# A recurrent attention and an MLP mixer on one core: the order of every engine's instructions planned inside the kernel instead of by the tile scheduler

## The chip, the cores and the metric

The kernel runs on one NeuronCore of a Trainium2 chip. The metric is the device time of one launch in microseconds (us). A time quoted here is a median over several runs. A run is labelled fast or slow: a run over 1.5% above the fastest run of the same kernel counts as slow, and only fast runs are compared. The time of the whole launch is about 2 us longer than the span of the trace, which begins at the first instruction (235.0 us against 233.0 for the kernel before).

The profile names the engines PE (matrix multiplications), PEld (loading of the stationary operand, overlaps PE), DVE (vector), ACT (scalar, activations), POOL (general purpose) and SP (sync, here only the issue of loads and stores). A name such as L242 is a line of the kernel. `SPq` and `POOLq` mark the issue of DMAs by SP and by POOL.

## The reference, cut to what matters

```python
# q, k, v, f_logit: (batch 4, heads 8, seq 768, head_dim 48), float32
f = 1.0 / (1.0 + np.exp(-f_logit))
for t in range(S):                                     # a recurrence over 768 positions
    state = f[:, :, t, :, None] * state + np.einsum('bhd,bhe->bhde', k[:, :, t], v[:, :, t])
    y[:, :, t] = np.einsum('bhd,bhde->bhe', q[:, :, t], state)

x = y.transpose(0, 2, 1, 3).reshape(B, S, 384)         # heads side by side
h = np.maximum(x.transpose(0, 2, 1) @ w_tok1, 0.0) @ w_tok2      # token mixing: 768 -> 256 -> 768
u = x + h.transpose(0, 2, 1)
return u + np.maximum(u @ w_ch1, 0.0) @ w_ch2          # channel mixing: 384 -> 1536 -> 384
```

Both kernels cut the sequence into six chunks of 128 positions. For each of the 24 pairs of batch and chunk they compute gates (exponentials and logarithms of `f_logit`), cumulative sums, the decayed q and k, scores within the chunk, a readout and an update of the state: this is called attention below. When all six chunks of a batch are read out, its mixing can start: two token matmul groups (12 matmuls with `w_tok1`, called the token matmuls below), then the matmuls with `w_tok2`, transposes, 72 matmuls with `w_ch1` and 72 with `w_ch2`. Attention of batch b+1 runs among the mixing of batch b.

## The kernel before

The parts that the change and the argument touch. The tile framework decides the order of each engine's instructions from the order in which they are emitted and from priorities; dependencies are found by it too.

```python
q_sb = two([128, H, NCH, D], BF16, "q_sb")            # two buffers each, used by batch b % 2
f_sb = two([128, H, NCH, D], FP32, "f_sb")            # likewise k_sb, v_sb

def load_f(b, eng, c=None):                           # one chunk, or all six in one DMA
    i = b % 2
    if c is None:
        eng.dma_start(out=f_sb[i], in_=tview(f_logit, b))
    else:
        eng.dma_start(out=f_sb[i][:, :, c, :], in_=tview(f_logit, b)[:, :, c, :])

def gates(b, c0, c1):                                 # three activations on ACT
    ...
    nc.scalar.activation(fb, fb, AF.Exp, bias=0.0, scale=-1.0)                            # L127
    nc.scalar.activation(Lhi[i][:, c0:c1, :, 0:D], fbc, AF.Ln, bias=1.0, scale=1.0)       # L128
    nc.scalar.activation(fb, fb, AF.Ln, bias=1.0, scale=1.0)                              # L129
    eng = nc.gpsimd if b else nc.vector
    eng.tensor_tensor(Llo[i][:, c0:c1, :, 0:D], fbc, Lhi[i][:, c0:c1, :, 0:D], ALU.subtract)   # L131

def readout(b, c):
    ...
    nc.scalar.copy(x_nat[i][:, c, :], py[:, 0:DM])
    (nc.gpsimd if b else nc.vector).tensor_copy(x_bf[i][:, c, :], x_nat[i][:, c, :])      # L187

# ... (front, scores, update, mixing: see the whole kernel)

for c in range(NCH):
    load_f(0, nc.sync, c)
for c in range(NCH):
    load_qkv(0, c)                                    # on POOL's queue, chunk by chunk
for w, src in ((w_tok1, moe_w_tok1), (w_tok2, moe_w_tok2), (w_ch1, moe_w_ch1), (w_ch2, moe_w_ch2)):
    nc.gpsimd.dma_start(out=w, in_=src.rearrange("(kt p) n -> p kt n", p=128))
load_f(1, nc.gpsimd)                                  # L279: whole batch, behind the weights
load_qkv(1)                                           # whole batch

for c in range(NCH):
    gates(0, c, c + 1)                                # all gates of batch 0 first on ACT
front(0, 0)
scores(0, 0)
front(0, 1)
for n, (b, c) in enumerate(steps):
    ...                                               # attention of one chunk, and a share of the
                                                      # mixing of the batch before among it
```

## Time and profile before

Four runs of the kernel before have a median of 232.71 us (230.48 to 234.62). The profiled execution took 235.0 us and counts as slow by the rule above, at a mean granted clock of 0.993, so no difference of less than about 2 us is read from its trace.

| stretch of the trace before | what limits it | PE busy |
|---|---|---|
| 0 to 45 us | loads, and in-order ACT with all gates of batch 0 first (the first decay exponential runs at 14.94 us) | 1.15, 2.77, 6.91, 8.01 us in the first four 10 us |
| 45 to 61 us | the `f_logit` load of batch 1, then what hangs on it | 1.12 us in 50 to 60 |
| from about 90 us | PE itself | nearly 10 us in each 10 us |

The head of the profile of the kernel before: busy tenths of each engine in 40 slices of 5.8 us, the granted clock of PE, and the busy share of the 16 DMA engines.

```profile
span 233.0 us, 4447 instructions
PE   0125778501379669999999999999999999999994
PEclk9999999999999997999999999999999999999999
DMA  8999999999999990009996000121000021100022
DMA packets 90292, 19.94 MB, mean 86 GB/s; under 512 B 80896, under 2 KB 89616, under 8 KB 90272
```

The hole in the PE row at slices 8 to 11 is the stall. The DMA engines are busy all the time until 87 us, with small packets: 90,292 packets for 19.94 MB. A load that is issued into this traffic lands late: `f_logit` of batch 1, issued behind the weights, takes 29.2 us from issue to landing.

The windows view of the kernel before. The columns are the stretch, its length, the busy us and instruction counts of PE, PEld, DVE, ACT and POOL, the granted clock, the DMA share and GB/s.

```profile
30.00:40.00 10.00, 8.01 (x79) 4.38 (x78) 6.47 (x18) 7.59 (x16) 1.76 (x1) 1.00 1.16 210
40.00:50.00 10.00, 4.25 (x42) 2.51 (x41) 5.96 (x16) 3.19 (x6) 0.00 (x0) 1.00 1.37 204
50.00:60.00 10.00, 1.12 (x13) 0.82 (x13) 2.63 (x1) 7.19 (x10) 6.78 (x4) 1.00 2.41 110
60.00:70.00 10.00, 6.51 (x60) 4.00 (x59) 5.56 (x10) 4.25 (x11) 7.00 (x4) 1.00 1.81 165
```

The chain of waits that ended last in the kernel before, in order of time: start, length, and what it was.

```profile
21.57 0.96 POOL w_ch_77 L278
22.53 29.18 DMA f_sb_85<-in_f_logit_dram
51.74 1.58 ACT f_sb_85 L127 x2
...
57.37 3.74 DVE x_bf_110 L187
...
79.99 0.66 PE pm L242 x3
...
117.47 0.97 PE pm L219 x6
...
159.50 0.97 PE pm L219 x6
...
199.04 1.96 PE pm L219 x12
...
229.70 0.55 DVE out_sb_119 L256
```

One DMA, `f_logit` of batch 1, stands in the chain for 29.18 us. It was issued behind the four weights on POOL's queue. The gates on ACT follow it, then a cast on DVE that takes 3.74 us. L242 at 79.99 us is the first channel matmul. L219 are the token matmuls of batches 1, 2 and 3: they mark the pace, 42 and 40 us per batch.

The list of waits of the kernel before in the stretch 30 to 80 us has the same load: total, times, longest.

```profile
ACT f_sb_85 L127 <- DMA f_sb_85<-in_f_logit_dram: 8.0, 1, 8.0
```

The timeline of DVE and of POOL around the slow cast, both of the kernel before:

```profile
57.37 3.73 DVE L187 CAST x_bf_110<-x_nat_108 128x384 bf16<-128x384 f32 x1 [9.91 <-ACT x_nat_108 L186]
57.64 4.95 POOL L131 TENSOR_TENSOR Llo_89<-f_sb_85,Lhi_87 128x768 bf16<-128x768 f32 x3
```

Alone the same cast takes 0.36 us, so beside three subtractions on POOL it takes ten times as long. Two multiplications of DVE, at 83.57 and 85.28 us, take 1.79 us each beside the next subtractions on POOL (81.80 to 88.57 us), and 0.36 us each alone. By what mechanism POOL's work slows DVE's is not shown.

### The profile page before, as it was taken

Reading aid. Unit: us, or ns where it says so; the run is one execution under the profiler, and the core shown is the slowest. Engines: PE = TensorE matmul, PEld = TensorE weight load, DVE = VectorE, ACT = ScalarE, POOL = GpSimd, SP = SyncE. Lnnn points to the kernel's source line nnn. Section 1 sums busy time; section 2 is a strip of 40 time slices with the busy share of each in tenths; the row PEclk is TensorE's granted clock in tenths of the full one; section 3 lists DMA queues with packets and bytes.
Section 4 is the critical chain, followed back from the end, with each engine's and each line's share of the span. In section 5 each row is a group of like instructions: output and inputs, shape, how many; then the busy total and the mean of one; then the engine's idle time right before and its main releaser. Section 6 shows DMA issues by size and latency. Waiting matters only on the chain.

```text
span 233.0 us, 4447 instructions
## 1 busy us (share of the span) xinstructions
PE 184.3 (79%) x1768; PEld 113.9 (49%) x1768; DVE 136.5 (59%) x283; ACT 114.8 (49%) x250; POOL 85.3 (37%) x115
## 2 busy tenths in 40 slices
PE   0125778501379669999999999999999999999994
PEld 0013445301245445666665666666665666455662
DVE  4145757711668796576668767756877762444221
ACT  5662394519254963762346774224766511165300
POOL 9979230008950596258245221201621221220000
PEclk9999999999999997999999999999999999999999
DMA  8999999999999990009996000121000021100022
GB/s 119 149 139 170 170 214 204 226 149 93 131 193 140 78 97 4 0 28 147 200 107 32 3 0 4 68 70 68 3 0 3 0 70 69 68 3 0 2 103 101
DMA packets 90292, 19.94 MB, mean 86 GB/s; under 512 B 80896, under 2 KB 89616, under 8 KB 90272
## 3 DMA queue, kind: packets, MB, share of 16 engines
q0 software_dynamic: 77472, 11.41, 78.9%
q1 hardware_dynamic: 12800, 8.26, 15.2%
q8 instruction: 14, 0.23, 0.5%
q14 instruction: 6, 0.05, 0.1%
HBM read 25.17 MB, written 4.72 MB: 128 GB/s over the span
## 4 chain that ended last, share of the span: by engine, by line
PE 60%; DMA 18%; ACT 7%; DVE 7%; POOL 6%; issue 1%; DVEq 0%; ACTq 0%; POOLq 0%
PE pm L242 20%; PE pm L253 18%; DMA f_sb_85<-in_f_logit_dram 13%; PE pm L226 4%; DMA k_sb_80<-in_k_dram 4%; PE pm L219 3%; ACT uT L236 3%; PE pq L158 2%; DMA out_dram<-out_sb_119 2%; PE pk L162 2%; ACT f_sb_85 L127 2%; DVE x_bf_110 L187 2%; POOL q_sb_78 L120 2%; PE py L178 1%; PE pd L196 1%; PE pS L139 1%
## 5 line engine op out<-in xcount | busy, mean ns | idle before, releaser
L242 PE MATMUL pm<-uT,w_ch_76 128*128 128x384 bf16 x288 | 55.1, 330 | 2.4 <-DVE zT L246 2.3
L253 PE MATMUL pm<-w_ch_77,zT 128*128 128x384 bf16 x288 | 50.6, 326 | 0.0
L248 ACT ACTIVATE zT<-pm 128x384 bf16<-128x384 f32 x56 | 27.5, 492 | 23.9 <-PE pm L242 23.8
L253 PEld LDWEIGHTS <-zT 128*128 128x128 bf16 x288 | 27.0, 98 | 16.7
L242 PEld LDWEIGHTS <-w_ch_76 128*128 128x128 bf16 x288 | 26.1, 98 | 17.9 <-issue 3.8
L246 DVE TENSOR_SCALAR zT<-pm 128x384 bf16<-128x384 f32 x40 | 21.2, 552 | 7.8 <-PE pm L242 7.5
L158 PE MATMUL pq<-ident,qh_94 128*128 128x128 bf16 x48 | 5.9, 249 | 11.3 <-DVE qh_94 L150 11.3
L146 ACT ACTIVATE G_90<-pS 128x384 bf16<-128x384 f32 x12 | 5.9, 488 | 15.2 <-PE pS L145 12.5
L219 PE MATMUL pm<-x_bf_110,w_tok_74 128*128 128x384 bf16 x24 | 7.2, 419 | 7.4 <-DVE x_bf_110 L187 6.4
L226 PE MATMUL pm<-h1T,w_tok_75 128*128 128x384 bf16 x48 | 12.2, 354 | 0.7 <-ACT h1T L221 0.5
L186 ACT COPY x_nat_109<-py 128x384 f32<-128x384 f32 x12 | 5.8, 482 | 12.9 <-PE py L183 11.8
L236 ACT CAST uT<-pm 128x384 bf16<-128x384 f32 x24 | 10.2, 488 | 3.6 <-PE pm L234 3.5
L118 POOL DMA_DIRECT2D k_sb_81<-in_k_dram x2 | 4.4, 2210 | 20.3 <-issue 20.3
L163 DVE CAST qkT_98<-pk 128x512 bf16<-128x512 f32 x12 | 8.3, 689 | 5.8 <-PE pk L162 5.8
L207 POOL CAST state_bd_106<-state_104 48x192 bf16<-48x192 f32 x9 | 3.1, 342 | 23.1 <-DVE state_104 L205 8.9
L138 PE MATMUL pS<-Lhi_87,tri_bf 128*128 128x384 bf16 x12 | 4.4, 371 | 8.8 <-ACT Lhi_87 L128 8.8
L187 DVE CAST x_bf_110<-x_nat_108 128x384 bf16<-128x384 f32 x6 | 5.5, 919 | 10.1 <-ACT x_nat_108 L186 9.9
L146 ACT ACTIVATE G_91<-pS 128x384 bf16<-128x384 f32 x12 | 5.8, 485 | 10.0 <-PE pS L145 10.0
L187 POOL CAST x_bf_111<-x_nat_109 128x384 bf16<-128x384 f32 x12 | 6.0, 503 | 12.5 <-ACT x_nat_109 L186 12.3
L158 PEld LDWEIGHTS <-qh_94 128*128 128x128 bf16 x48 | 3.8, 110 | 13.0 <-DVE qh_94 L150 11.9
L131 POOL TENSOR_TENSOR Llo_89<-f_sb_85,Lhi_87 128x768 bf16<-128x768 f32 x6 | 9.9, 1671 | 0.1
L234 PE MATMUL pm<-ident,u_bf 128*128 128x128 bf16 x72 | 7.5, 218 | 3.1 <-ACT uT L236 1.8
(217 smaller groups left out, 411.5 us busy)
## 6 DMA issues: line engine op xcount, KB each, us to landing
out_dram<-out_sb_118 SPq DMA_DIRECT2D x12, 192.0 KB, 1.9
out_dram<-out_sb_119 SPq DMA_DIRECT2D x12, 192.0 KB, 1.9
f_sb_84<-in_f_logit_dram SPq DMA_DIRECT2D x6, 192.0 KB, 5.5
w_ch_76<-in_moe_w_ch_dram POOLq DMA_DIRECT2D x1, 1152.0 KB, 18.8
w_ch_77<-in_moe_w_ch_dram POOLq DMA_DIRECT2D x1, 1152.0 KB, 23.9
f_sb_85<-in_f_logit_dram POOLq DMA_DIRECT2D x1, 1152.0 KB, 29.2
q_sb_79<-in_q_dram POOLq DMA_DIRECT2D x2, 576.0 KB, 17.3
k_sb_81<-in_k_dram POOLq DMA_DIRECT2D x2, 576.0 KB, 10.2
```

The lines of the kernel that those rows point to most:

```text
L131: eng.tensor_tensor(Llo[i][:, c0:c1, :, 0:D], fbc, Lhi[i][:, c0:c1, :, 0:D], ALU.subtract)
L146: nc.scalar.activation(G[j].rearrange("t h d -> t (h d)"), Sv, AF.Exp, bias=0.0, scale=-1.0)
L158: nc.tensor.matmul(pq[:, hp * 128:(hp + 1) * 128], lhsT=qb[:, hp, :], rhs=ident, start=True, stop=True)
L163: nc.vector.tensor_copy(qkT[j][:, 4:8, :], pk.rearrange("p (a t) -> p a t", a=4))
L187: (nc.gpsimd if b else nc.vector).tensor_copy(x_bf[i][:, c, :], x_nat[i][:, c, :])
L219: nc.tensor.matmul(pm[:, 0:DM], lhsT=w_tok1[:, kt, rt * 128:(rt + 1) * 128], rhs=x_bf[i][:, kt, :], start=(kt == 0), stop=(kt == NCH - 1))
L226: nc.tensor.matmul(pm[:, 0:DM], lhsT=w_tok2[:, kt, tt * 128:(tt + 1) * 128], rhs=h1T[:, kt, :], start=(kt == 0), stop=(kt == 1))
L236: nc.scalar.copy(uT[:, :, tt * 128:(tt + 1) * 128], pm[:, 0:DM].rearrange("p (m t) -> p m t", m=3))
L242: nc.tensor.matmul(pm[:, 0:384], lhsT=w_ch1[:, kt, cc * 128:(cc + 1) * 128], rhs=uT[:, kt, th * 384:(th + 1) * 384], start=(kt == 0), stop ...
L246: nc.vector.tensor_scalar(dst, pm[:, 0:384], 0.0, None, ALU.max)
L248: nc.scalar.activation(dst, pm[:, 0:384], AF.Relu, bias=0.0, scale=1.0)
L253: nc.tensor.matmul(pm[:, 0:DM], lhsT=zT[:, kt, tt * 128:(tt + 1) * 128], rhs=w_ch2[:, kt, :], start=(kt == 0), stop=(kt == NCC - 1))
```

## The change

The intent: the kernel lists all operations with the engines that may do them, an assumed duration, their dependencies and a key (a wished time). A small list scheduler inside the kernel then simulates the engines, PSUM banks and one serial DMA queue, and gives one order. The instructions are emitted in that order with the tile scheduler's reordering switched off (`tc.manual_schedule()`). The framework still inserts the semaphores. Along with it come other changes: q, k, v and f_logit are loaded chunk by chunk for every batch, the layout of their tiles has the chunk outermost, gates alternate with attention, most casts go to DVE or ACT instead of POOL, and `w_ch2` is loaded after five chunks of batch 1 (`W2 = 5`).

The diff, cut to its core:

```diff
+class Plan:
+    LATE = {"PE": 0.32, "ACT": 0.24, "DVE": 0.24, "POOL": 0.3, "SP": 0.1, "Q": 2.0}   # visible to others after
+    BANKS = {"att": 5, "mix": 3}
+    def add(self, engines, fn, key, deps=(), bank=None, frees=None, at=0.0, banks=1): ...
+    def order(self):
+        queues = {e: sorted((o for o in self.ops if e in o["eng"]), key=lambda o: o["key"])
+                  for e in ("PE", "ACT", "DVE", "POOL", "SP", "Q")}
+        ...                      # again and again: the operation that can start first, ties by key
-    q_sb = two([128, H, NCH, D], BF16, "q_sb")
-    f_sb = two([128, H, NCH, D], FP32, "f_sb")
+    q_sb = two([128, NCH, H, D], BF16, "q_sb")
+    f_sb = two([128, NCH, H, D], FP32, "f_sb")
+    def load_f(b, c, key, at=0.0):
+        i = b % 2
+        deps = [made.get(("lo", b - 2, c))]            # the last reader of this buffer
+        if b:
+            def token(e):                              # makes the load wait for DVE's place in the order
+                nc.vector.memset(f_sb[i][0:1, c, 0, 0:1], 0.0)
+            deps = [add({"DVE": 0.06}, token, key, deps, at=at)]
+        def issue(e):
+            nc.sync.dma_start(out=f_sb[i][:, c], in_=chunk_of(f_logit, b, c))
+        n = add({"SP": 0.1}, issue, key, deps, at=at)
+        made["f", b, c] = add({"Q": 1.1}, None, key, [n])        # 1.1 us on a serial queue
+    def load_qkv(b, c, key, at=0.0):
+        ...                                            # POOL 0.89 us to issue, 0.72 us on the queue
+    def gates(b, c0, c1, key):
+        ...
+        o = add({"POOL": 0.85 * n} if b > 1 else {"DVE": 0.4 * n + 0.08},
+                lambda e: on(e).tensor_tensor(lo, fb, hi, ALU.subtract), key, [g, h])
+    def attention(b, c, key, at=0.0):
+        p2 = (b, c - 2) if c >= 2 else (b - 1, c + NCH - 2)      # the last user of these buffers
+        ...
+            made["bd", b, c] = add({"DVE": 0.5, "ACT": 0.5}, diag, key + 0.02, [s_, made.get(("y", *p2))])
+        ...
+        made["xb", b, c] = add({"DVE": 0.28, "ACT": 0.4}, ...)   # was POOL from batch 1 on
-    load_f(1, nc.gpsimd)
-    load_qkv(1)
+    W2 = 5
+    PACE = (34.0, 5.6)
+    for c in range(NCH):
+        load_f(0, c, 0.1 * c)
+        load_qkv(0, c, 0.1 * c)
+    ...                                                # w_tok1, w_tok2, w_ch1
+    for c in range(NCH):
+        if c == W2:
+            load_w("w_ch2", w_ch2, moe_w_ch2, 0.63 + 0.01 * c, 6.0)
+        load_f(1, c, 0.63 + 0.01 * c, at=24.0 + 2.0 * c + (6.0 if c >= W2 else 0.0))
+        load_qkv(1, c, 0.63 + 0.01 * c)
+    for c in range(NCH):
+        gates(0, c, c + 1, 0.1 * c)
+        attention(0, c, 0.1 * c + 0.1)
+    for b in range(B):
+        if b + 1 < B:
+            for c in range(NCH):
+                if b >= 1:
+                    load_f(b + 1, c, b + 0.05 + 0.1 * c)
+                    load_qkv(b + 1, c, b + 0.05 + 0.1 * c)
+            ...                                        # gates and attention of batch b + 1
+        mixing(b, b + 1.0, 1.0)
+    order = plan.order()
+    with tc.manual_schedule():
+        for t, e, o in order:
+            if o["fn"] is not None:
+                o["fn"](e)
```

## The prediction

> **What bounds the kernel now.** Three stages.
>
> (1) Start, 0 to 45 us. The windows view shows PE 1.15, 2.77, 6.91 and 8.01 us busy in the first four 10 us windows. ACT works in order and has all six gate groups of batch 0 first, so the first decay exponential runs at 14.9 us and PE's first transposes at 15.9 us, though q, k, v take only about 8 us to land.
>
> (2) A stall, 45 to 61 us: PE busy 1.12 us in 50 to 60. The chain of waits names it: the f_logit load of batch 1, one DMA behind the four weights on POOL's queue, takes 29.2 us and lands at 51.7; ACT has been idle for 8.0 us in front of it; then five 128x768 gate activations, then an x_bf cast on DVE that takes 3.73 us (0.36 alone) while three Llo subtractions take 4.95 us on POOL. [...] (qh_95 and kh_97 also take 1.7 us beside POOL, 0.36 alone). Mixing of batch 0 is late by all this.
>
> (3) From about 90 us PE is the limit: busy 98 to 100% of each window to 200 us. Batches follow at 42 and 40 us (token matmuls at 117.5, 159.5, 199.0 in the chain).
>
> **What the change does.** PE's work stays. In dense stretches three channel matmuls take 0.49 us, twelve 1.95: 28.4 us of mixing per batch (estimate: 174 matmuls at 0.163 plus transposes), and attention about 2.0 us per chunk ((81.6 - 2x28.4)/12). Sum 162 us.
> - Gates are interleaved with the chunks: batch 0 attention starts about 5 us sooner.
> - f_logit of batch 1 comes by chunk on SP's queue, so ACT is not blocked: stage (2), about 16 us, goes.
> - q, k, v of batch 1 come by chunk before w_ch2. Bytes and small packets stay; the DMA row is full until 87 us now. [...] So channel matmul 2 of batch 0 cannot start before about 60 us.
> - x_bf, u_bf and state_bd casts leave POOL for DVE or ACT: some 7 us per batch, where DVE and ACT are 67% and 50% busy in 120 to 200.
> - Steady state gains little: PE was full already; 0 to 2 us a batch.
>
> **Sum.** Token matmuls of batch 0 end at about 37 us (62 now), its channel matmuls begin at 41 to 43 (80 now), token matmuls of batch 1 at 75 to 80 (117.5 now). Then about 109 us of PE work (4 left over, 85 mixing, 20 attention), some 6 us of gaps and 3 us of output tail: about 197 us, 16% less. Chances: faster 0.95, same 0.03, slower 0.02.
>
> **What would show it.** No ACT wait of more than 3 us for batch 1's f_logit; PE at least 70% busy in 40 to 60; first channel matmul near 42 us; batch periods still 39 to 42 us; PE busy sum falling to 170 to 180.
>
> **What would make it wrong.** The order is fixed by assumed durations and serial DMA. If loads land later (f_logit of batch 2 is issued early and competes with q, k, v of batch 0), in-order engines block on the wrong instruction: slower, to 210. If w_ch2 lands after 65 us PE idles. If attention of batch 0 ends at 30 us: below 190.

75 to 80 us, then 109, 6 and 3 us, come to 193 to 198 us, put at about 197. The 60 us for channel matmul 2 rest on the full DMA row alone and are the author's estimate.

## The result, and the profile after

The changed kernel takes 216.91 us (median of four runs, 215.31 to 217.47), the kernel before 232.71 us. The ratio is 0.934, with a 95% interval from 0.924 to 0.944. A ratio in this document is the mean time of one kernel's fast runs over that of the other's fast runs of the same rounds, so it is not quite the ratio of the quoted medians. The change is faster, by 6.6%, but the predicted 197 us are missed, and so are the 210 us that the prediction gave for loads that land later.

The head of the profile of the changed kernel, to be read against the one above:

```profile
span 215.3 us, 4558 instructions
PE   0525789588999597978989999998999999899993
PEclk9999999976999889996999999999999999999999
DMA  7999999999999999999979002210000132000032
DMA packets 106326, 19.96 MB, mean 93 GB/s; under 512 B 100288, under 2 KB 105920, under 8 KB 106304
```

The long hole of PE is gone. But the DMA row stays full until about 118 us instead of 87 us, in one piece. There are 16,000 more packets for the same 20 MB: the loads by chunk bring all of `f_logit` in pieces of 192 bytes, where before that held for batch 0 alone, and the others came in pieces of 768 or 4,224 bytes. The clock row has new dips.

The windows view of the changed kernel:

```profile
30.00:40.00 10.00, 8.37 (x87) 5.13 (x85) 6.83 (x22) 7.09 (x18) 1.97 (x3) 1.00 1.31 179
40.00:50.00 10.00, 7.06 (x54) 4.04 (x55) 6.36 (x19) 6.76 (x17) 4.38 (x5) 0.81 1.78 136
50.00:60.00 10.00, 10.00 (x106) 5.76 (x105) 8.25 (x23) 8.59 (x23) 4.50 (x5) 0.85 1.72 136
...
70.00:80.00 10.00, 7.53 (x66) 4.40 (x64) 4.77 (x12) 4.03 (x10) 4.38 (x5) 0.83 1.97 143
```

Between 40 and 60 us PE is busy for 17.06 us, against 5.37 us before. Part of that is the same work done slowly: the granted clock is 0.81 to 0.85 in three of the four stretches shown (the trace before has 1.00 in its four, but its clock records begin only at 74.5 us). And there is a new weak stretch from 70 to 80 us.

The chain of waits of the changed kernel:

```profile
6.16 11.41 DMA v_sb_82<-in_v_dram
...
23.93 13.63 DMA w_ch_76<-in_moe_w_ch_dram
37.84 16.27 DMA k_sb_81<-in_k_dram
54.41 19.22 DMA w_ch_77<-in_moe_w_ch_dram
73.68 2.10 PE pm L452 x6
...
83.18 1.72 DVE state_108 L335
...
97.47 3.73 PE pm L384 x12
...
141.34 1.97 PE pm L384 x12
...
181.95 1.31 PE pm L384 x7
...
211.91 0.55 DVE out_sb_123 L461
```

Up to 73.68 us most of the chain is four loads, one behind another; the chain before had the 29.18 us load and, at the start, a load of k of 8.47 us. `w_ch2` (`w_ch_77`) lands at 73.6 us, where the prediction had about 60. The token matmuls of batch 1 (L384) start at 97.47 us, 20 us sooner than before, but at 75 to 80 in the prediction. From there to the end it takes 117.8 us of trace (215.3 less 97.5); before it was 115.5 (233.0 less 117.5), and the prediction's sum has 118. So the whole miss of 20 us lies before the token matmuls of batch 1.

What stood at 73 us, in the list of waits of the changed kernel for 60 to 80 us:

```profile
ACT G_90 L272 <- PE pS L266: 5.2, 1, 5.2
DVE qh_94 L281 <- ACT G_90 L272: 4.1, 1, 4.1
...
PE pm L452 <- DMA w_ch_77<-in_moe_w_ch_dram: 2.5, 1, 2.5
```

PE waits for `w_ch2` for only 2.5 us. But behind that matmul in PE's fixed order stands the cumulative sum of batch 1, chunk 4 (it starts at 75.58 us), and ACT waits 5.2 us for it, and DVE 4.1 us: with a fixed order one late load stops attention too, which did not need it. PE is also at half its clock here (granted 0.50, in a record of 3.4 us from 73.5 us on): the first six matmuls with `w_ch2` take 2.10 us, where six take about 0.98 us later.

Who kept the DMA engines busy? The timeline of SP, of the changed kernel: the issue of `f_logit` loads, `f_sb_84` being batches 0 and 2, `f_sb_85` batches 1 and 3.

```profile
0.75 33.30 SPq L211 DMA_DIRECT2D f_sb_84<-in_f_logit_dram  x11
34.10 3.44 SPq L211 DMA_DIRECT2D f_sb_85<-in_f_logit_dram  x1
37.64 2.06 SPq L211 DMA_DIRECT2D f_sb_84<-in_f_logit_dram  x1
39.76 33.80 SPq L211 DMA_DIRECT2D f_sb_85<-in_f_logit_dram  x11
```

By 34 us SP has issued eleven loads of `f_sb_84`: six of batch 0 and five of batch 2, which ACT first uses at 79.1 us. By 73.5 us batch 3 is issued as well. Of these twelve loads of batches 2 and 3 (1,024 packets of 192 bytes each) seven are issued before `w_ch2` is, at 54.4 us, and beside the q, k, v loads of batches 0 and 1; the other five are issued while `w_ch2` is under way. The plan allows it: as soon as the gates have used a chunk of `f_sb`, the next but one batch may be loaded into it, SP is idle, and the plan's single serial queue has holes.

### The profile page after: what moved, and what is told of

It is laid out like the page before. It is cut to its first block, busy times and chain, and to the rows that moved or that the text cites. A ratio compares the mean times of both kernels' runs of the same rounds, so it can differ in the third digit from the quotient of the medians.

```text
span 215.3 us, 4558 instructions
## 1 busy us (share of the span) xinstructions
PE 182.8 (85%) x1768; PEld 112.8 (52%) x1768; DVE 134.7 (63%) x317; ACT 141.7 (66%) x315; POOL 77.5 (36%) x90
## 2 busy tenths in 40 slices
DMA packets 106326, 19.96 MB, mean 93 GB/s; under 512 B 100288, under 2 KB 105920, under 8 KB 106304
## 4 chain that ended last, share of the span: by engine, by line
PE 52%; DMA 28%; DVE 6%; ACT 5%; POOL 5%; issue 2%; DVEq 0%; POOLq 0%
PE pm L452 21%; PE pm L433 16%; DMA w_ch_77<-in_moe_w_ch_dram 9%; DMA k_sb_81<-in_k_dram 8%; DMA w_ch_76<-in_moe_w_ch_dram 6%; DMA v_sb_82<-in_v_dram 5%; PE pm L384 3%; POOL k_sb_80 L228 2%; PE pm L403 1%; DVE u_nat_118 L407 1%; POOL q_sb_78 L228 1%; POOL v_sb_82 L228 1%; PE pk L292 1%; PE pq L292 1%; ACT u_bf L189 1%
## 5 line engine op out<-in xcount | busy, mean ns | idle before, releaser
L452 PE MATMUL pm<-w_ch_77,zT 128*128 128x384 bf16 x288 | 53.3, 331 | 2.5 <-DMA w_ch_77<-in_moe_w_ch_dram 2.5
L433 PE MATMUL pm<-uT,w_ch_76 128*128 128x384 bf16 x288 | 53.0, 330 | 0.0
L195 ACT ACTIVATE zT<-pm 128x384 bf16<-128x384 f32 x78 | 37.9, 503 | 4.1 <-PE pm L433 3.8
L433 PEld LDWEIGHTS <-w_ch_76 128*128 128x128 bf16 x288 | 26.7, 98 | 16.1 <-issue 0.7
L461 DVE TENSOR_TENSOR out_sb_122<-u_nat_118,pm 128x384 f32<-128x384 f32 x6 | 3.3, 550 | 17.5 <-PE pm L452 17.4
L228 POOL DMA_DIRECT2D k_sb_80<-in_k_dram x12 | 10.7, 888 | 9.1 <-DMA w_ch_77<-in_moe_w_ch_dram 6.5
L228 POOL DMA_DIRECT2D k_sb_81<-in_k_dram x12 | 10.8, 898 | 8.7 <-DMA w_ch_76<-in_moe_w_ch_dram 5.3
L228 POOL DMA_DIRECT2D v_sb_83<-in_v_dram x12 | 10.8, 903 | 5.7 <-DMA q_sb_79<-in_q_dram 4.2
L228 POOL DMA_DIRECT2D q_sb_79<-in_q_dram x12 | 10.9, 912 | 4.3 <-DMA k_sb_81<-in_k_dram 2.4
L228 POOL DMA_DIRECT2D q_sb_78<-in_q_dram x12 | 10.9, 906 | 3.7 <-DMA k_sb_80<-in_k_dram 1.3
L228 POOL DMA_DIRECT2D v_sb_82<-in_v_dram x12 | 10.7, 896 | 3.5 <-DMA q_sb_78<-in_q_dram 1.4
L197 DVE TENSOR_SCALAR zT<-pm 128x384 bf16<-128x384 f32 x18 | 9.6, 551 | 3.2 <-PE pm L433 3.0
L189 ACT COPY x_nat_112<-py 128x384 f32<-128x384 f32 x11 | 5.3, 478 | 9.3 <-PE py L352 8.5
L384 PEld LDWEIGHTS <-w_tok_74 128*128 128x128 bf16 x48 | 5.2, 114 | 7.4 <-issue 6.0
L189 ACT COPY x_nat_113<-py 128x384 f32<-128x384 f32 x9 | 4.4, 492 | 6.8 <-PE py L352 6.8
L407 DVE TENSOR_TENSOR u_nat_118<-x_nat_113,pm 128x384 f32<-128x384 f32 x12 | 6.1, 546 | 3.9 <-PE pm L403 3.9
```

Source lines behind the costliest of these rows:

```text
L189: nc.scalar.copy(dst, src)
L195: nc.scalar.activation(dst, src, AF.Relu, bias=0.0, scale=1.0)
L197: nc.vector.tensor_scalar(dst, src, 0.0, None, ALU.max)
L228: lambda e, dst=dst, src=src: nc.gpsimd.dma_start(out=dst[i][:, c], in_=chunk_of(src, b, c)),
L384: nc.tensor.matmul(t["p"][:, 0:DM], lhsT=w_tok1[:, kt, rt * 128:(rt + 1) * 128], rhs=x_bf[i][:, kt, :], start=(kt == 0), stop=(kt == NCH - 1))
L407: u = made["u", b, tt] = add({"DVE": 0.47}, lambda e, tt=tt, t=t: nc.vector.tensor_tensor(u_nat[i][:, tt, :], x_nat[i][:, tt, :], t["p"][: ...
```

## The experiments

The theories are named as the expectations name them. Theory A: the early `f_logit` loads of batches 2 and 3 take DMA time from what is needed next. Its rivals: B, PE's slow matmuls at the start and the latency of the chain of chunks cost the time (in the changed kernel 384-column matmuls are 0.29 to 0.32 us apart before 35.9 us and 0.162 us later; the texts call this the cold or slow clock, but the trace has no clock record before 35.9 us); C, `w_ch2` is simply placed too late (`W2 = 5`); D, POOL's subtractions slow DVE down (1.7 us for an operation that takes 0.36 us alone). A further question is what part of the gain comes from the fixed order and what part from the rest, such as the loads by chunk. Every edit of the kernel makes the plan anew, so the order of operations that were not edited can change with it. Twelve runs were made, in three batches on three chips. Where kernels of different batches are compared, it is by their ratios to the kernel before.

| kernel | median us (lowest, highest) | ratio to before | correct |
|---|---|---|---|
| changed kernel | 216.91 (215.31, 217.47) | 0.934 | yes |
| 1 late f_logit loads | 208.72 (206.20, 209.65) | 0.890 (two fast runs) | yes |
| 2 w_ch2 first | 217.91 (215.69, 218.90) | 0.9348 | no |
| 3 the same again | 219.19 (one run) | | no |
| 4 w_ch2 first, dependency added | 214.96 (213.03, 216.07) | 0.9218 | yes |
| 5 order left to the tile scheduler | 224.52 (223.65, 225.52) | 0.9647 | yes |
| 6 kernel before, f_logit of batch 1 on SP | 234.16 (232.53, 235.26) | 1.0054 | yes |
| 7 f_logit in whole batches | 224.09 (223.38, 225.01) | 0.9618 | yes |
| 8 run 1, subtractions on DVE | 206.74 (205.69, 207.10) | 0.8864 | yes |
| 9 run 8, f_logit of batch 0 paced | 205.56 (205.32, 206.36) | 0.8832 | yes |
| 10 run 9, PE kept busy | 205.71 (204.41, 212.59) | 0.8811 | yes |
| 11 run 9, dependency added | 207.39 (206.88, 207.81) | 0.8901 | yes |
| 12 run 9, order left to the tile scheduler | 217.99 (217.41, 218.40) | 0.9355 | yes |

In the second and third batch (runs 4 and 7 to 12; run 3 is a single run and has no verdict) the recorded verdict reads "unclear" although the intervals of the ratios, about 0.006 to 0.011 to either side, lie far from 1; two of the seven runs of the kernel before were classed slow there. For run 1 two of its four runs count as slow (209.37 and 209.65 us); 0.890 is the mean of its two fast runs (207.1 us) over the mean of the six fast runs of the kernel before in that batch (232.8 us).

### Run 1: the f_logit loads of batches 2 and 3 later

```diff
-                    load_f(b + 1, c, b + 0.05 + 0.1 * c)
+                    load_f(b + 1, c, b + 0.05 + 0.1 * c, at=(52.0 if b == 1 else 76.0) + 3.2 * c)
```

> Only change: the f_logit loads of batches 2 and 3 are held until the time at which the plan itself serves them (52 us and 76 us plus 3.2 us a chunk), instead of being issued by SP as soon as their buffer is free (from 6 us on). Theory A (early f_logit loads steal packets from q, k, v of batches 0 and 1 and from w_ch2): the last token matmul of batch 0 comes at 38 to 40 us (41.9 in the changed kernel), w_ch2 lands before 67 us (73.6), PE does not wait for it, and the time is 207 to 211 us (216.9). Rival B (the slip is the cold PE clock and the latency of the chunk chain, not the order of loads): within 1.5 us of 216.9.

Measured: 208.72 us, ratio 0.890, so 8 to 10 us faster than the changed kernel. The last token matmul of batch 0 runs at 38.1 us instead of 41.9, the first channel matmul at 45.73 instead of 51.16, the first with `w_ch2` at 64.92 instead of 73.68, with no wait for it. Its chain of waits has hardly a load left. By engine, the changed kernel's chain and then that of run 1:

```profile
PE 52%; DMA 28%; DVE 6%; ACT 5%; POOL 5%; issue 2%; DVEq 0%; POOLq 0%
```

```profile
PE 59%; DVE 22%; ACT 9%; DMA 4%; issue 3%; POOL 2%; DVEq 0%; POOLq 0%
```

DMA falls from 28% of the chain to 4%. PE's first 481 operations of 1,768, up to about 60 us, are the same in both traces, so the 4 and 5 us gained by then do not come of another order on PE; after that the orders differ. What follows: theory A holds, and it is the largest single piece of the miss. The rival B, which expected no more than 1.5 us, is not the main cause. The token matmuls of batch 1 begin at 86.09 us, so half of the lateness against the predicted 75 to 80 goes, half stays.

### Runs 2, 3 and 4: w_ch2 in front of batch 1

```diff
-    W2 = 5
+    W2 = 0
```

> Only change: w_ch2 is issued before all q, k, v loads of batch 1 instead of before those of chunk 5. If the place of w_ch2 alone costs what the prediction lost (theory C), PE no longer waits for it near 71 us and the time falls to 210 to 213 us. Theory A says the total of DMA packets is what counts: w_ch2 lands by 52 us, but q, k, v of batch 1 land 10 us later, attention of batch 1 is late, and the time is 215 to 222 us.

Measured: 217.91 us, no gain, and a wrong result, with a relative error of 0.0619. `w_ch2` is no longer waited for, but q, k, v and f_logit of batch 1 come later by as much: the first transposes of batch 1 run at 57.4 us instead of 48.5. So the place of `w_ch2` alone is not the fault: theory C expected 210 to 213 us. Too much traffic in front of either load would explain it.

The wrong result was not expected. First, whether it is a chance event:

> The same kernel as e2, once more, only to see whether its wrong result comes again. A fault in the kernel that this order brings out would come again; a rare event would not. Time 215 to 219 us.

The error came again, the same to the last digit, at 219.19 us. So it is fixed by the order, not by timing. Comparing the order with the list of dependencies showed what is missing: `state_bd` has two buffers; the cast of chunk c writes buffer c % 2, and the readout of chunk c reads buffer (c - 1) % 2. So before the cast of chunk c writes, the readout of chunk c - 1 must have read that same buffer. The plan lists the readout of chunk c - 2 instead. In the order of the changed kernel the right sequence happens to hold everywhere; with `W2 = 0` the cast comes before the readout for batch 2, chunk 2, and for batch 3, chunk 0. The check for races cannot find this: with a fixed order the emitted sequence is the meaning of the program, and the semaphores then keep the wrong sequence faithfully.

```diff
-            made["bd", b, c] = add({"DVE": 0.5, "ACT": 0.5}, diag, key + 0.02, [s_, made.get(("y", *p2))])
+            made["bd", b, c] = add({"DVE": 0.5, "ACT": 0.5}, diag, key + 0.02,
+                                   [s_, made.get(("y", b, c - 1) if c else ("y", b - 1, NCH - 1))])
```

> e2 (w_ch2 before the loads of batch 1) plus one dependency that the plan's list lacks: the cast into state_bd of chunk c waits for the readout of chunk c-1, which still reads the tile's older value. e2's plan puts that cast in front of the readout twice (batch 2 chunk 2, batch 3 chunk 0); the changed kernel's never does. If this is why e2 gave a wrong result, e11 is correct. Time as e2: 215 to 220 us.

Measured: correct, 214.96 us, ratio 0.9218. The missing dependency is the cause. The ratio lies 0.012 under that of the changed kernel, with intervals that overlap (0.911 to 0.933 and 0.924 to 0.944): not told apart.

### Run 5: the changed kernel without the fixed order

```diff
-    with tc.manual_schedule():
-        for t, e, o in order:
-            if o["fn"] is not None:
-                o["fn"](e)
+    for t, e, o in order:
+        if o["fn"] is not None:
+            o["fn"](e)
```

> The changed kernel with the same loads, layouts, engines and order of emission, but without the fixed order: the tile scheduler may move instructions again. If the fixed order is what gives the gain over the kernel before, this falls back to 225 to 233 us. If the gain comes from the split loads and the order of emission, it stays within 3 us of 216.9.

Measured: 224.52 us, ratio 0.9647. This is neither of the two times expected, but near the first. So of the 6.6% gain about 3.5% stay without the fixed order (loads by chunk, layout, engines, order of emission), and about 3.1%, some 7 us, are lost with it. The fixed order therefore has a part in the gain. But it fixes two things, the order of compute and the time at which loads are issued, and this run lets both go: by 30 us it has issued 16 loads of `f_logit` where the changed kernel has issued ten, and `w_tok1` lands at 41.7 us instead of 29.1. Run 12 comes back to this.

### Run 6: the kernel before, with only f_logit of batch 1 moved to SP's queue

```diff
-    load_f(1, nc.gpsimd)
+    load_f(1, nc.sync)
```

> The kernel before with one line changed: f_logit of batch 1 is issued on SP's queue (right after batch 0's) instead of last on POOL's. Theory A: the stall of 45 to 61 us, whose start is this load, shrinks by about 8 us of ACT wait; q, k, v of batch 0 come some 2 us later; the time is 222 to 228 us, so a third to two thirds of the gain of the change is this one load. Rival: q, k, v of batch 1 are then the next thing to be late on the same DMA engines, and the time stays at 230 to 233 us.

Measured: 234.16 us, ratio 1.0054 (0.997 to 1.014): no gain. The load that the chain named as the stall no longer stalls, and the kernel is as slow as ever. Its chain of waits shows who pays:

```profile
6.12 12.14 DMA v_sb<-in_v_dram
18.55 16.21 DMA k_sb<-in_k_dram
...
40.52 16.75 issue
```

The early load on the other queue now delays q, k, v of batch 0 and all that is behind them on POOL's queue. That is not the whole of it: the 16.75 us of "issue" are a time in which POOL stands at its loads of batch 1 for a reason that the profile does not show, and POOL's subtractions of batch 1 start only after it, at 59.5 us. The kernel before has such a wait too, of 20.3 us. What it costs here was not tested. The pages of the profile count both queues on the same 16 DMA engines (in the kernel before POOL's takes 78.9% and SP's 15.2% of those engines' time), and in run 6 POOL's queue falls to 1,026 packets in 5 us beside SP's, from 7,338 alone in run 1. Counting the profile's packets in the traces:

| kernel and stretch | POOL's queue, packets of 96 B | SP's queue, packets |
|---|---|---|
| run 1, 15 to 20 us, POOL's queue alone | 7,338 | none |
| changed kernel, 45 to 50 us | 2,730 | 2,153 of 192 B |
| changed kernel, 50 to 55 us | 2,542 | 2,235 of 192 B |
| run 6, 15 to 20 us | 1,026 | 1,035 of 768 B |
| run 7, 35 to 40 us | 1,029 | 1,042 of 768 B |

In these stretches the two queues go nearly packet for packet: 1.1 to 1.3 of POOL's to one of 192 bytes, one to one with those of 768 bytes (the kernel before has 618 to 618 in 22 to 25 us). By what rule they do so is not shown. An estimate from these counts: a q, k or v chunk (1,024 packets) that takes 0.7 us alone (5 us x 1,024 / 7,338) takes about 2.0 us beside 192-byte pieces and 5 us beside 768-byte pieces. The plan had 0.72 us for it, and one queue in which the loads come strictly after each other.

### Run 7: f_logit of batches 1 to 3 in one DMA each

```diff
-    f_sb = two([128, NCH, H, D], FP32, "f_sb")
+    f_sb = two([128, H, NCH, D], FP32, "f_sb")
...
+            if b:
+                nc.sync.dma_start(out=f_sb[i], in_=f_logit[b].rearrange("h (c t) d -> t h c d", t=C))
+            else:
+                nc.sync.dma_start(out=f_sb[i][:, :, c, :], in_=chunk_of(f_logit, b, c))
```

> The changed kernel with f_logit of batches 1 to 3 loaded in one DMA each, in the layout of the kernel before (768-byte packets there, 192-byte packets in the changed kernel), still issued as soon as the buffer is free. If the number of small packets is what the early loads cost (theory A2), 13,800 packets fewer bring as much as holding the loads back did (8 us): 207 to 211 us, w_ch2 before 67 us. If only the early issue matters, it stays at 214 to 218 us.

Measured: 224.09 us, ratio 0.9618, so 3.0% slower than the changed kernel where a gain was expected if the 192-byte pieces were the fault, and outside both of the times expected. There are fewer packets, but POOL's queue moves fewer of its own beside them (1,029 in 5 us in the last line of the table above, 2,542 to 2,730 beside those of 192 bytes), and a whole batch has to land before its first chunk can be used: ACT waits 6.2 us for `f_logit` of batch 1 again. So joining the small pieces is no cure in this form. How much the number of pieces costs by itself this run cannot say, since it changed three things at once: their size, when the first chunk can be used, and when the buffer is free for the load. Run 1 has the same 106,326 packets as the changed kernel and is 8 to 10 us faster: there only the time at which they are sent was edited.

### Run 8: run 1, and the subtraction Llo of batches 2 and 3 on DVE

```diff
-        o = add({"POOL": 0.85 * n} if b > 1 else {"DVE": 0.4 * n + 0.08},
+        o = add({"DVE": 0.4 * n + 0.08},
```

> e1 (late f_logit loads) plus: the Llo subtractions of batches 2 and 3 run on DVE (0.88 us planned) instead of POOL (1.7 us). If POOL's subtraction slows the DVE operations beside it (1.7 us instead of 0.36) and this is on the chain at 85 and 95 us (theory D), it is 2 to 4 us faster than e1 (208.7): 205 to 207 us. Rival: DVE, 66% busy, only takes more work, and the time is within 1 us of e1 or above.

Measured: 206.74 us, ratio 0.8864, against 0.890 of run 1's two fast runs. The medians differ by 2.0 us, the ratios by less than 1 us. What theory D supposes is visible in the traces (a state update of the changed kernel at 83.18 us takes 1.72 us beside a subtraction on POOL, 0.36 us at 103.06), but its worth in time is not settled by these runs; it is at most about 2 us.

### Run 9: run 8, and f_logit of batch 0 paced

```diff
-        if b:
+        if b or at:
...
-        load_f(0, c, 0.1 * c)
+        load_f(0, c, 0.1 * c, at=2.6 * c if c > 1 else 0.0)
```

> e7 plus: the f_logit loads of batch 0's chunks 2 to 5 are issued at 5 to 13 us instead of all at once at the start. If they delay q, k, v of the first chunks by sharing the DMA engines (theory A at the start), the last token matmul of batch 0 moves from 38.1 us in e1 to 36 or 37 us and the time is 1 to 3 us below e7. Rival: all 24 loads of batch 0 are needed in any order before the last chunk can start, so nothing changes (within 1 us).

Measured: 205.56 us (205.32 to 206.36), ratio 0.8832 (0.876 to 0.890), correct. This is the fastest version: 11.7% under the kernel before, and 5.1% of that kernel's time under the changed kernel. The last token matmul of batch 0 runs at 36.8 us, as expected. Against run 8 of the same batch it gains 1.2 us of median with overlapping spreads, so the rival (within 1 us) is not excluded. The head of its profile:

```profile
span 203.2 us, 4569 instructions
PE   0787887799999999678999999989999998899993
DMA  8999999999999999999970022100001122000132
```

PE works from the second slice on. The DMA row is as full as before, until about 110 us: it is the same traffic, in an order in which the next thing needed comes next.

### Run 10: run 9, with PE kept busy

Before each PE operation of batch 0's attention stand four more 128x128 matmuls whose result is never used.

```diff
+    def heat(b):
+        if b == 0:
+            ...
+            for _ in range(4):
+                nc.tensor.matmul(warm[0][:, 0:128], lhsT=ident, rhs=ident, start=True, stop=True)
```

> e9 plus four matmuls of 128x128 into an unused bank in front of each PE operation of batch 0's attention, which keep PE busy while it waits for loads. If the slow clock of the first 35 us (384-column matmuls 0.3 us apart instead of 0.16) costs time (rival B), the last token matmul of batch 0 moves from 36.8 us to 34 to 36 us and the time is 1 to 3 us below e9 (205.6). If loads set the pace there, it is within 1 us of e9 or slower.

Measured: 205.71 us, ratio 0.8811: the same as run 9. The matmuls did become faster: the timeline of PE has the first seven token matmuls of batch 0, in run 9 and in run 10 in turn, as

```profile
28.32 2.42 PE L384 MATMUL pm<-x_bf,w_tok 128*128 128x384 bf16 x7
```

```profile
28.73 1.31 PE L398 MATMUL pm<-x_bf,w_tok 128*128 128x384 bf16 x7
```

so 1.31 us instead of 2.42 us. But the last two of them start at 36.05 us instead of 36.52 us. So keeping PE busy in this way gains nothing that can be measured in the total, which fits a start at which PE waits for data. The added matmuls take PE time too; whether that hides a small gain was not tested. What the traces of the two kernels show of the clock: the records grant 1.00 or 0.50, and matmuls of the same shape are 0.16 us or 0.32 us apart. In the changed kernel four records of 0.50 in the span last 3.4 us each; the windows of run 9 add up to twice that length from 30 to 50 us. The one at 42.7 us begins although PE was busy for 1.64 us of the 3.41 us before, with no pause longer than 1.1 us. Before the first record, at 35.9 us, the profile shows 1.00, but 384-column matmuls there are 0.29 to 0.32 us apart, so that 1.00 does not describe them. What makes the clock fall is not shown.

### Run 11: run 9, with the missing dependency

The same edit of the dependency as in run 4, on run 9.

> e9 plus the missing dependency of e11: the version that stays right under any order. Another plan comes of it, but nothing in it is longer: 204 to 208 us.

Measured: 207.39 us, ratio 0.8901, correct. It is the version to use: the plan cannot break it when a key or a duration is altered. Its plan comes out a little different and is about 1.8 us slower in the medians; the intervals of the two ratios overlap (0.884 to 0.896 and 0.876 to 0.890).

### Run 12: run 9, without the fixed order

The same edit as in run 5, on run 9.

> e9 without the fixed order: the tile scheduler moves instructions again. In the changed kernel the fixed order was worth 7.6 us (224.5 in e4 against 216.9). If the tile scheduler's early loads were most of that, the difference shrinks to 2 to 5 us: 207 to 211 us. If the order of compute is what counts, it stays 7 us or more: 212 us or above.

Measured: 217.99 us, ratio 0.9355, so 12.4 us more than run 9 in the medians. I expected the fixed order to be worth little once the loads are in good order. The run does not test that, because without the fixed order the loads are not in good order any more: the times at which `f_logit` is held back are part of the planned order. By 30 us this run has issued 14 loads of `f_logit` and run 9 eight; `w_tok1` is issued at 22.8 us instead of 17.5 and lands at 38.2 us instead of 25.4. The list of waits for 20 to 45 us has the wait that comes of it:

```profile
PE pm L384 <- DMA w_tok<-in_moe_w_tok_dram: 12.4, 1, 12.4
```

In the tile scheduler's order the first token matmul of batch 0 stands early on PE, and attention of the later chunks stands behind it while `w_tok1` is missing (PE is busy for 1.77 us in 30 to 40 us, and the first attention matmuls run again at 38.5). In run 5 the same wait is 8.3 us long, and the fixed order was worth 7.6 us in medians there:

```profile
PE pm L384 <- DMA w_tok<-in_moe_w_tok_dram: 8.3, 1, 8.3
```

The planned order has that matmul at 28.3 us in run 9, when the weight is there. So in both cases the worth of the fixed order is about the size of this one wait. That is an agreement of sizes: no run took this wait alone away, and none kept the loads of the plan while it freed the order of compute. How the worth divides between the two stays open.

## Why the prediction was right or wrong

**Right: the direction, and the stall.** The 45 to 61 us stall is gone: PE is busy 71% and 100% of 40 to 50 and 50 to 60 us, as predicted (at least 70%). The longest wait of ACT for `f_logit` of batch 1 before 60 us is 1.6 us (predicted below 3).

**Right: nothing gained in the steady state.** From the token matmuls of batch 1 to the end it takes 117.8 us of trace; the sum predicted 118. The batches follow at 43.9 and 40.6 us (predicted 39 to 42; in the first, the token matmuls at its start run at half clock: twelve take 3.73 us, in the next batch 1.97).

**Half right: the start.** Batch 0's first transposes come 7.7 us sooner (8.13 us, before 15.86; predicted about 5). But the token matmuls of batch 0 end at 42.2 us instead of 37, because the gain is eaten on the way: loads of later chunks arrive late (in run 1, with the late `f_logit` loads held back, the last of these matmuls comes at 38.1 us). This is 5 us of the miss.

**Wrong: "its channel matmuls begin at 41 to 43".** They begin at 51.16 us. Of the 8 to 10 us, 5 are the lateness of the token matmuls; the rest is between them and the channel matmuls, 9 us from 42.2 to 51.2 where I had 4 to 6, with PE at a granted clock of 0.50 in two records of 3.4 us (at 42.7 and 49.6 us).

**Wrong, and the step that failed: "q, k, v of batch 1 come by chunk before w_ch2. Bytes and small packets stay ... So channel matmul 2 of batch 0 cannot start before about 60 us".** I counted the bytes before `w_ch2` as those of the kernel before in another order. But before it or beside it go `f_logit` of batches 2 and 3, and all of `f_logit` comes in 192-byte pieces: 106,326 packets, not 90,292. `w_ch2` landed at 73.6 us, 13 us late. Run 1, whose edit only holds those loads back, lands `w_ch2` at 58.1 us, brings its first use to 64.9 us and takes 8 to 10 us off the total, with the same number of packets. So the step failed by when these loads go; that their number costs anything by itself is not shown. I had named the risk ("f_logit of batch 2 is issued early and competes with q, k, v of batch 0") and given it a bound of 210 us; it was not a risk but visible in the plan, and worth more than I gave it.

**The term that was mis-sized: "token matmuls of batch 1 at 75 to 80".** They began at 97.5 us, and all 20 us of the miss (216.9 less 197.0) lie before them: about 5 at the token matmuls of batch 0, about 4 more at its first channel matmul, the other 11 between there and the token matmuls of batch 1. In those 11 are PE's wait for `w_ch2`, attention of batch 1 blocked behind that wait in the fixed order (ACT 5.2 us), and DVE operations beside POOL. Runs 1, 8 and 9 take away the causes in DMA and POOL and bring the mark to 84.7 us. What is left, 5 to 10 us, is not settled. In run 9 DVE is busy for 54.2 us and PE for 54.3 us of the 60 us from 40 to 100 us, so there both are near their limit; I had looked at DVE's room only in the steady state.

**Wrong in its reason: "f_logit of batch 1 comes by chunk on SP's queue, so ACT is not blocked".** The stall did go in the changed kernel, but run 6 shows that another queue alone gives nothing (1.0054). I had written that bytes and small packets stay, and did not follow it to the end: there the load that came earlier made others come later (a v load of batch 0 lands 12.1 us after its issue, against a median of 7.7 in the kernel before, and POOL's queue falls to 1,026 packets in 5 us, from 7,338 alone).

**Missed: what the fixed order is worth.** The prediction gave the gain to the loads and the gates, and none to the fixed order as such. Runs 5 and 12 put it at 7 and 12 us, and the wait in the traces that fits both sizes is the one for `w_tok1`, which lands 12.7 and 12.8 us later without the fixed order. How much of this is the order of the loads and how much that of compute is not shown.

**Wrong, small: "PE busy sum falling to 170 to 180".** It was 182.8 us (184.3 before). Four records of 3.4 us at a granted 0.50 in the changed kernel against one before fit this, but the records before begin only at 74.5 us, so it is not shown.

## What to carry to other kernels

When a chain of waits names a load, look at what is in front of it on all queues before you move it: in run 6 a load that started earlier on another queue left the one that was needed then 1,026 packets in 5 us instead of 7,338, the stall moved to that, and the time stayed (ratio 1.0054). Hold loads for later stages back until the DMA engines have nothing more urgent; here that one edit was worth 8 to 10 us. A planned order was worth 7 and 12 us here, and it set when loads were issued as well as the order of compute; to learn which of the two pays, one has to be kept while the other is freed. With a planned order the list of dependencies is the program: check each buffer's last reader, as the check for races did not find the missing line here.
